# Fold amid block 8's products, an earlier load into its place, and four batches stored as whole rows

## Chip, cores and metric

One core of one Trainium2 chip runs the whole program. Time is device microseconds (us) of one execution; lower is better. The kernel before takes 438.74 us (median of three runs, 438.12 to 438.96).

## The reference

Three stages, all float32. x is 8 batches x 8 heads x 512 tokens x 64, state has 32 slots for each batch and head. Cut to what matters:

```python
# 1. attention both ways between tokens and state slots
a  = softmax(x @ state.T / 8);  xread = a @ state
a2 = softmax(state @ x.T / 8);  sread = a2 @ x
x  = concat([xread, sread], axis=2)          # 544 rows a batch, 4352 in all, 512 wide
# 2. dense layer
x = silu(x @ w_in) @ w_out                   # 512 -> 2048 -> 512
# 3. soft mixture: 8 experts x 4 slots
logits = x @ phi
d = softmax(logits, axis=0)                  # over all 4352 rows
slot_in = d.T @ x                            # 32 slots
slot_out[e] = relu(slot_in[e] @ w1[e]) @ w2[e]
out = softmax(logits, axis=1) @ slot_out     # 4352 x 512
```

The last softmax over rows and the slots need every row, so the experts run after the last block, and the result after the experts.

## The kernel before

**Blocks.** Blocks 0 to 7 are one batch's 512 tokens each; block 8 is the 256 state rows. For each block `hid` (or `hid8`, block 8) makes the hidden layer in pieces of 128 columns (tiles `h` in PSUM), ACT applies SiLU, `logits` or `logits8` multiplies with a folded matrix `w2p` (tile `lg`), and `s_rep`, `s_dTg` add the block's weighted hidden rows (`S`) into the sum `acc`, 128 x 4 x 512 in SBUF. In block 8 the weights come as high and low parts `wc`, made piece by piece by ACT, DVE and POOL from `win`, and the products are `h <- wc, rd`; `gt` are its transposes for `logits8`.

**The joint.** `join7` finds the minimum over rows after block 7 (tile `top`) and puts its factor into `r4e[:, 0]`. `sum7` scales the sum (tile `sum`). `fold` multiplies `acc` by `r4e` into 128 x 512 (four products, eight matmul records), and ACT copies it to `accX`. `rep8` does block 8's minimum (`lg8t`), exp (into `thb`) and transposes (`dT`). Then `slot_acc`, `slot_T` and `slot_mm` (tiles `siT`, `si`) make the slots' input from `accX` and block 8's `S`.

**Experts.** `f` are the products with w1 (two passes), `hT` their transposes, `so` the products with w2, once for each half of the 512 result columns. 32 tiles of 1 MB, 16 of w1 and 16 of w2, are loaded into places that earlier work leaves: `places` lists them (raw blocks, `win`, `g`, `acc`, `wb`, ...), `at_place` says which tile goes where, and `load_w(n)` issues the loads up to number n. `acc` is place 12. In `at_place` it holds tile 17, the second one of w2, and is loaded after `fold`.

**Result.** For each half of the columns `sor` is made from `so`, and `out_tiles` multiplies it with the softmax weights `cT` (tiles `o`, four for each batch), copies them to SBUF (DVE the even, ACT the odd), and `store` sends a batch out. `HALVES` are the batches whose first 256 columns are stored while the second half's `so` is still at work: all nine, so each batch leaves as two stores with rows of 1 KB (`outb[q, 0:512, cols]`).

**Order.** No engine runs in the order in which the code is written. `Recorder` records each instruction; `schedule` plays them through with planned durations and always takes the one of least priority number (place in the code plus `nc.shift` plus a number of the table `RANK`). SP issues all transfers in one queue, in that planned order, and at most eight are under way: an issue waits until the transfer eight before it has landed. In two stretches (`FILL`) the planner puts dummy products of `cst` into gaps of TensorE.

Of the kernel before, what the change touches and what calls it, by code (L numbers as in the profile page):

```python
# [15 lines left out]
NB = 8  # L16
# [30 lines left out]

LATE = {"in_w_out": 3.0, "wo_f32": 3.0, "in_xT_dr": 1.5, "in_xk_dr": 1.5}

LG8 = -450  # L50
FOLD = 0
# [18 lines left out]
HALVES = (0,1,2,3,4,5,6,7,NB)  # L70
# [44 lines left out]
    ("7", "ACT", "activation", "m", 0): 581,  # L115
    ("7", "ACT", "activation", "thb", 1): 1500,
    ("7", "ACT", "activation", "wo", 1): -857,
    ("7", "DVE", "transpose", "src", 0): 73,
    ("7", "DVE", "transpose", "src", 1): 200,
    ("7", "DVE", "transpose", "src", 3): 30,  # L120
    ("7", "DVE", "transpose", "src", 6): 1181,
    ("7", "PE", "matmul", "h", 8): 565,
    ("7", "PE", "matmul", "lg", 2): 1500,
    ("7", "PE", "matmul", "lg", 12): 1028,
    ("7", "PE", "matmul", "wbp", 0): 1474,
    ("7", "PE", "matmul", "wbp", 2): 615,
    ("8", "ACT", "copy", "wc", 5): -507,
    ("8", "DVE", "tensor_copy", "g", 0): -62,
    ("8", "DVE", "tensor_copy", "place", 0): -366,
    ("8", "DVE", "tensor_copy", "thb", 2): 991,  # L130
    ("8", "PE", "matmul", "S", 5): -333,
    ("8", "PE", "matmul", "dT", 0): 1251,
    ("8", "PE", "matmul", "f", 11): 823,
    ("8", "PE", "matmul", "f", 13): -209,
    ("8", "PE", "matmul", "h", 3): 119,
    ("8", "PE", "matmul", "h", 9): -974,
    ("8", "PE", "matmul", "h", 14): -745,
    ("8", "PE", "matmul", "lg", 4): 1500,
    ("8", "PE", "matmul", "o", 5): -14,
    ("8", "PE", "matmul", "o", 7): 948,  # L140
    ("8", "PE", "matmul", "si", 1): -1389,
    ("8", "PE", "matmul", "si", 2): -1381,
    ("8", "PE", "matmul", "si", 3): -562,
    ("8", "PE", "matmul", "so", 18): -193,
    ("8", "PE", "matmul", "so", 19): -442,
    ("8", "PE", "matmul", "so", 23): -570,
    ("8", "PE", "transpose", "dT", 0): 1161,
    ("8", "PE", "transpose", "gt", 9): 1042,
    ("8", "PE", "transpose", "gt", 10): 1014,
    ("8", "PE", "transpose", "hT", 0): 827,  # L150
# [69 lines left out]
class Recorder:  # L220
# [189 lines left out]
    def schedule(self):  # L410
# [44 lines left out]
        while n_left:  # L455
# [48 lines left out]
            if e == PE and any(lo <= busy[PE] < hi for lo, hi in FILL):  # L504
                at = max(busy[PE], self.filling[1])
                n = int((st - at - (0.2 if fills else 2.2)) / FILLER)
                room = []
                for tag in free:
                    if tag.split("_")[1] == "ps" and tag[0] != "h" and free[tag] and qpos[tag] < len(queue[tag]):
                        room.append((*min(free[tag]), tag))  # L510
                if n > 0 and room and min(room)[0] <= at:
                    _, old, tag = min(room)
                    order.append(self.filler(queue[tag][qpos[tag]], old, n, at))
                    fills += 1
                    mode, run = FULL, 0
# [8 lines left out]
            elif e == SP:  # L524
                op.start = st
                busy[SP] = st + op.cost
                t0 = max(st + op.cost + 0.9, dma_free)
                dma_free = t0 + op.bytes / DMA_RATE
                end = dma_free + 1.1
                landed.append(end)  # L530
                end += op.tail
            else:
                if e == ACT and op.mode is not None and table not in op.mode:
                    st += 1.3
                    table = op.mode[0]
                op.start = st
                busy[e] = st + op.cost
                end = st + op.cost + op.tail
                if e == DVE:
                    tailed = op  # L540
                    if op.port:
                        busy["port"] = end
                end += 0.04
# [66 lines left out]
def tile_state_attention_soft_moe(  # L610
# [557 lines left out]
    def rep8():  # L1168
# [5 lines left out]
        nc.after(fold_op[0], mm(p[:, 0:256], lhsT=r44, rhs=x, start=True, stop=True))  # L1174
# [110 lines left out]
    at_place = [0, 1, 2, 3, 4, 5, 6, 7, 8, 10, 9, 11, 13, 14, 15, 16, 17, 12, 18, 19, 20, 21, 22, 23] + [0, 1, 2, 3, 4, 5, 6, 8]  # L1285
# [41 lines left out]
    fold_op = []  # L1327

    def fold():

        p = bank("h", "fold")
        with nc.together():
            for q in range(4):
                op = mm(p[32 * q:32 * q + 32, :], lhsT=r4e[:, 0], rhs=acc[:, q], start=True, stop=True)
        fold_op[:] = [op]
        x = rot.tile([128, 512], F32, tag="wf", name="accX", bufs=1)
        nc.scalar.copy(out=x, in_=p)
        return x
# [178 lines left out]
    for fq in range(4):  # L1517
        hid8(fq)
        if fq == 0:
# [15 lines left out]
            s_dTg(NB - 1)  # L1535
            nc.shift = 0
# [4 lines left out]
        if fq == 1:  # L1541
# [6 lines left out]
            load_w(12)  # L1548
        if fq == 2:
            for n in range(12, 16):  # L1550
                split_w(n)
            load_w(13)
        if fq:
            logits8(fq - 1)
    load_w(16)
    logits8(3)
    load_w(17)
# [3 lines left out]

    nc.shift = FOLD
    accX = fold()
    load_w(18)
# [143 lines left out]
    todo = [*HALVES, *(q for q in range(NB + 1) if q not in HALVES)]  # L1708
# [56 lines left out]
```

## Time and profile before

| | us |
|---|---|
| median of three runs (lowest, highest) | 438.74 (438.12, 438.96) |
| the profiled execution, its time | 438.37 |
| its span, first to last instruction | 436.6 |
| TensorE busy (PE) | 414.4 (95%) |
| VectorE (DVE) | 291.9 (67%) |
| ScalarE (ACT) | 283.7 (65%) |
| GpSimd (POOL) | 119.2 (27%) |
| HBM read, written | 79.37 MB, 12.06 MB |

All numbers below come from this one execution. PE is the matmuls and PEld the loads of their weights. SPq is SyncE's queue of transfers, the time at which it issues one; "to landing" runs from there until the data is there. A matmul product in float32 shows as two records. The chain of waits follows the work that ended last back from the end; each piece is the time until the next piece takes over. PEclk is TensorE's granted clock as a share of 2.4 GHz. `L571` is the helper line that issues every instruction, so the tiles' names tell the instructions apart.

### The profile page before, as it was taken

What the parts mean: (1) busy time and instruction counts of PE and PEld (TensorE: products, weight loads), DVE (VectorE), ACT (ScalarE), POOL (GpSimd) and SP (SyncE); (2) the same over time, 40 slices, a digit from 0 to 9 for tenths busy, and PEclk for the clock granted to TensorE, in tenths of its full rate; (3) what the DMA queues carried; (4) which work ended last, traced back from release to release, by engine and by line L of the source; (5) the groups of instructions that cost most, each with busy time, mean ns of one, the idle gap of its engine ahead of it and who ended that gap; (6) DMA issues with size and microseconds to landing.
All of it is one profiled execution on the core that took longest, in us unless ns stands there. A gap on an engine that the chain in (4) does not pass through costs nothing.

```text
span 436.6 us, 10970 instructions
## 1 busy us (share of the span) xinstructions
PE 414.4 (95%) x4536; PEld 273.3 (63%) x4536; DVE 291.9 (67%) x548; ACT 283.7 (65%) x512; POOL 119.2 (27%) x71
## 2 busy tenths in 40 slices
PE   8889999999999999999999999999999999999980
PEld 5555657766856775785776677577677685435530
DVE  3989999883797598479659748943965544221460
ACT  4999997756688788679777657666876455011360
POOL 0024332044137135434714511441353130000000
PEclk9999999999999999999999999999999999999996
DMA  8999941238779998888896767465699988999998
GB/s 324 425 423 424 376 150 65 98 73 197 212 224 262 244 269 262 225 250 255 251 257 216 183 189 210 100 141 139 218 417 331 340 345 313 421 426 427 401 381 284
DMA packets 37890, 117.31 MB, mean 269 GB/s; under 512 B 3408, under 2 KB 12496, under 8 KB 29776
## 3 DMA queue, kind: packets, MB, share of 16 engines
q1 hardware_dynamic: 37840, 116.60, 79.3%
q8 instruction: 36, 0.59, 0.5%
q14 instruction: 14, 0.11, 0.1%
HBM read 79.37 MB, written 12.06 MB: 209 GB/s over the span
## 4 chain that ended last, share of the span: by engine, by line
PE 81%; DMA 8%; ACT 6%; DVE 2%; issue 0%; DVEq 0%; SPq 0%
PE h L571 44%; PE lg L571 7%; PE S L571 6%; PE wbp L571 6%; DMA raw<-in_w_in_dram 4%; PE so L571 3%; PE f L571 3%; DMA src<-in_w_out_dram 2%; PE o L571 2%; PE eT L571 1%; PE sc L571 1%; PE sr L571 1%; ACT L571 1%; DMA xT<-in_xT_dram 1%; PE si L571 1%; ACT g L571 1%
## 5 line engine op out<-in xcount | busy, mean ns | idle before, releaser
L571 PE MATMUL h<-ar,wb 128*128 128x512 f32 x768 | 189.6, 399 | 2.0 <-ACT g L571 2.0
L571 PEld LDWEIGHTS h<-ar,wb 128*128 128x128 f32 x768 | 140.2, 188 | 47.4 <-ACT g L571 6.4
L571 DVE STREAM_TRANSPOSE src<-g 128x512 f32<-128x512 f32 x112 | 78.0, 703 | 36.9 <-ACT g L571 31.9
L571 ACT ACTIVATE g<-h 128x512 f32<-128x512 f32 x100 | 58.9, 610 | 28.4 <-PE h L571 24.8
L571 POOL TENSOR_TENSOR wb<-wf,wb 128x512 fp32r<-128x512 f32 x26 | 33.8, 1299 | 111.4 <-ACT wb L571 89.7
L571 ACT CAST wb<-wbp 128x512 fp32r<-128x512 f32 x64 | 35.5, 594 | 10.4 <-PE wbp L571 9.6
L571 PEld LDWEIGHTS lg<-g,w2p 128*32 128x32 f32 x1072 | 28.1, 109 | 21.2 <-issue 16.8
L571 PE MATMUL lg<-g,w2p 128*32 128x128 f32 x1072 | 37.2, 275 | 0.2 <-DVE g L571 0.2
L571 POOL TENSOR_TENSOR s<-s,tm 128x1024 f32<-128x1024 f32 x12 | 23.3, 1941 | 43.0 <-DVE tm L571 35.9
L571 PE MATMUL wbp<-win,ss 64*32 64x512 f32 x512 | 33.3, 597 | 1.5 <-DVE win L571 1.1
L571 PE MATMUL S<-dst,dT 128*32 128x512 f32 (+1 forms) x328 | 28.4, 595 | 0.0
L571 ACT ACT_TABLE_LOAD x21 | 26.9, 1283 | 1.1 <-PEq L1755 0.7
L571 DVE TENSOR_TENSOR wb<-wbp,wb 128x512 fp32r<-128x512 f32 x38 | 24.9, 662 | 2.5 <-ACT wb L571 2.5
L571 ACT ACTIVATE thb<-h 128x512 f32<-128x512 f32 x30 | 17.9, 600 | 12.4 <-PE h L571 12.0
L571 DVE SCALAR_TENSOR_TENSOR g<-thb,h 128x512 f32<-128x512 f32 x28 | 18.9, 680 | 7.9 <-ACT thb L571 6.0
L571 PE MATMUL h<-wc,rd 128*128 128x512 f32 x96 | 24.0, 401 | 0.0
L571 DVE SCALAR_TENSOR_TENSOR acc<-acc,m,S 128x512 f32<-128x512 f32 x28 | 20.4, 736 | 4.3 <-PE S L571 3.8
L571 PE MATMUL lg<-thb 128*128 128x256 f32 x72 | 19.3, 415 | 1.2 <-DVE thb L571 1.2
L571 DVE TENSOR_REDUCE tm<-s 128x32 f32<-128x1024 f32 (+1 forms) x18 | 19.5, 1090 | 1.0 <-ACT s L571 0.8
L571 PEld LDWEIGHTS h<-wc,rd 128*128 128x128 f32 x96 | 17.5, 188 | 4.0 <-issue 0.2
L571 DVE TENSOR_REDUCE asm<-e 128x2 f32<-128x1024 f32 x8 | 9.6, 1203 | 15.3 <-ACT e L571 15.3
L571 PEld LDWEIGHTS lg<-thb 128*128 128x128 f32 x72 | 14.2, 205 | 5.7 <-issue 2.5
(190 smaller groups left out, 600.7 us busy)
## 6 DMA issues: line engine op xcount, KB each, us to landing
dst<-src SPq DMA_DIRECT2D x96, 256.0 KB, 4.8
place<-in_w_dram SPq DMA_DIRECT2D x12, 1024.0 KB, 9.6
xT<-in_xT_dram SPq DMA_DIRECT2D x8, 1024.0 KB, 8.6
raw<-in_w_in_dram SPq DMA_DIRECT2D x8, 1024.0 KB, 11.8
xk<-in_xk_dram SPq DMA_DIRECT2D x8, 1024.0 KB, 8.2
raw<-in_w_outT_dram SPq DMA_DIRECT2D x8, 1024.0 KB, 8.4
src<-in_w_out_dram SPq DMA_DIRECT2D x6, 1024.0 KB, 8.4
dst<-in_w_dram SPq DMA_DIRECT2D x6, 1024.0 KB, 12.3
```

Of the source, the lines that this page charges most:

```text
L571: made = [call(*args, **kwargs) for call, args, kwargs in op.calls]
```

## The change

`FOLD`, the shift that put `fold` after block 8, goes. `fold` is now recorded within `hid8`'s first round, after `s_dTg(NB - 1)`, and in the PSUM bank tag `w` instead of `h`. `at_place` exchanges two entries, so that `acc` holds tile 11 (of w1) and is loaded with the pieces of `win`; the tiles behind it move up by one place, and the numbers of `load_w` follow. `HALVES` becomes batches 0 to 3 and the state rows' part NB. In the planner a free stretch after 100 us is filled with dummies up to its end, and loads of over 0.9 MB after 250 us are planned to take 3 us longer. `RANK` has other numbers for blocks 7 and 8 (36 entries become 20).

```diff
+REST = 3.0
-FOLD = 0
-HALVES = (0,1,2,3,4,5,6,7,NB)
+HALVES = (0, 1, 2, 3, NB)
...
-    ("8", "PE", "transpose", "hT", 0): 827,
+    ("8", "PE", "matmul", "top", 0): 868,
...
-                n = int((st - at - (0.2 if fills else 2.2)) / FILLER)
+                n = int((st - at + 0.1) / 0.43) if st > 100 else int((st - at - (0.2 if fills else 2.2)) / FILLER)
...
-                t0 = max(st + op.cost + 0.9, dma_free)
+                t0 = max(st + op.cost + 0.9 + REST * (op.bytes > 9e5 and not op.tail and st > 250), dma_free)
...
-        nc.after(fold_op[0], mm(p[:, 0:256], lhsT=r44, rhs=x, start=True, stop=True))
+        mm(p[:, 0:256], lhsT=r44, rhs=x, start=True, stop=True)
...
-    at_place = [0, 1, 2, 3, 4, 5, 6, 7, 8, 10, 9, 11, 13, 14, 15, 16, 17, 12, 18, 19, 20, 21, 22, 23] + [0, 1, 2, 3, 4, 5, 6, 8]
+    at_place = [0, 1, 2, 3, 4, 5, 6, 7, 8, 10, 9, 12, 11, 13, 14, 15, 16, 17, 18, 19, 20, 21, 22, 23] + [0, 1, 2, 3, 4, 5, 6, 8]
...
     def fold():
-        p = bank("h", "fold")
+        p = bank("w", "fold")
...
             s_dTg(NB - 1)
+            nc.shift = -6 * FIRST
+            accX = fold()
             nc.shift = 0
...
-    nc.shift = FOLD
-    accX = fold()
-    load_w(18)
...
-    todo = [*HALVES, *(q for q in range(NB + 1) if q not in HALVES)]
+    todo = [*HALVES[:2], *(q for q in range(NB + 1) if q not in HALVES), *HALVES[2:]]
```

TensorE after block 7's part of S (not shown), in block 8, before; `h` are the hidden products, in threes:

```order
L571 MATMUL top_697<-fin,cst 128x4
L571 MATMUL h_1_1_707<-wc_677,rd 128x512 x3
L571 MATMUL h_1_1_707<-wc_686,rd 128x512 x6
L571 MATMUL gt_0_0_710<-cst,dst 128x128 x4
L571 MATMUL gt_0_1_711<-cst,dst 128x128 x4
L571 MATMUL h_2_0_714<-wc_677,rd 128x512 x3
L571 MATMUL h_2_1_715<-wc_677,rd 128x512 x3
L571 MATMUL gt_1_0_716<-cst,dst 128x128 x2
L571 MATMUL sum_708<-fin,cst 128x1
```

And in the same place now:

```order
L556 MATMUL h_1_1_709<-wc_686,rd 128x512 x3
L556 MATMUL h_1_0_708<-wc_686,rd 128x512 x3
L556 MATMUL h_1_1_709<-wc_686,rd 128x512 x3
L556 MATMUL top_697<-fin,cst 128x4
L556 MATMUL gt_0_0_712<-cst,dst 128x128 x4
L556 MATMUL gt_0_1_713<-cst,dst 128x128 x4
L556 MATMUL h_2_0_716<-wc_677,rd 128x512 x3
L556 MATMUL fold<-acc,r4e 32x512 x4
L556 MATMUL h_2_0_716<-wc_677,rd 128x512 x3
L556 MATMUL sum_710<-fin,cst 128x1
```

`fold` stands between products of `h_2_0`, and `top`, on which its factor rests, comes nine products later after S than before.

SP's queue at the end of the loads into `win`, before:

```order
L571 DMA win_80<-in_w_dram 128x512 x3
L571 DMA win_81<-in_w_dram 128x512 x4
L571 DMA place_724<-in_w_dram 128x2048
L571 DMA place_725<-in_w_dram 128x2048
L571 DMA place_726<-in_w_dram 128x2048
...
L571 DMA w2p<-in_w_dram 128x512
L571 DMA acc<-in_w_dram 128x2048
```

And now:

```order
L556 DMA win_80<-in_w_dram 128x512 x2
L556 DMA acc<-in_w_dram 128x2048
L556 DMA win_81<-in_w_dram 128x512 x4
L556 DMA place_726<-in_w_dram 128x2048
L556 DMA place_727<-in_w_dram 128x2048
L556 DMA place_728<-in_w_dram 128x2048
```

The load into `acc` moved ahead of eleven other loads.

TensorE from the second round of `so` to the first results of the last half, now (before, five pieces of `so_806` stood between 36 tiles `o` of the first half):

```order
L556 MATMUL o_0_3_789<-thb,win_79 64x256
L556 MATMUL so_790<-place_660,src 32x256 x8
L556 MATMUL so_790<-place_661,src 32x256 x8
L556 MATMUL so_790<-place_687,src 32x256 x8
L556 MATMUL so_790<-win_78,src 32x256 x8
L556 MATMUL so_790<-src 32x256 x16
L556 MATMUL sor_792<-sos_791,cst 128x256
L556 MATMUL o_256_0_793<-thb,win_79 128x256
```

The 20 tiles `o` of the first half all stand ahead of the last 48 products of `so`. After them come two half batches, then batches 4 to 7 as whole rows (`o` of 128x512, stores of `128x4x512`, 2 KB a row), then the other halves.

## Rows read from the trace of the kernel before

**Rows 1.** Page, part 2: mean busy share of the transfer engines in 40 slices

```profile
DMA  8999941238779998888896767465699988999998
```

**Rows 2.** Windows: length; PE, PEld, DVE, ACT, POOL busy; PEclk, transfer share, GB/s

```profile
357.00:366.00 9.00, 8.35 (x99) 6.71 (x98) 2.38 (x4) 3.64 (x6) 0.00 (x0) 1.00 0.70 239
360.00:361.00 1.00, 1.00 (x6) 0.77 (x6) 0.00 (x0) 0.15 (x1) 0.00 (x0) 1.00 0.01 4
361.00:362.00 1.00, 1.00 (x8) 0.86 (x7) 0.00 (x0) 0.34 (x1) 0.00 (x0) 1.00 0.88 197
378.00:408.00 30.00, 28.99 (x354) 12.60 (x350) 7.10 (x13) 5.25 (x12) 0.00 (x0) 1.00 1.01 425
410.00:411.00 1.00, 1.00 (x23) 0.64 (x24) 1.00 (x4) 0.69 (x3) 0.00 (x0) 1.00 0.98 366
411.00:432.00 21.00, 12.83 (x156) 5.65 (x144) 9.56 (x27) 8.85 (x27) 0.00 (x0) 0.92 1.09 382
```

**Rows 3.** Timeline of SP's queue: start us, us spent issuing, what

```profile
360.25 5.92 SPq L571 DMA_DIRECT2D place<-in_w_dram  x6
...
367.75 0.39 SPq L571 DMA_DIRECT2D acc<-in_w_dram  x1
...
404.64 0.40 SPq L571 DMA_DIRECT2D out_dram<-win  x1
...
419.67 0.42 SPq L571 DMA_DIRECT2D out_dram<-acc  x1
```

**Rows 4.** Transfers issued in 393 to 394 and 419 to 420: size, us to landing

```profile
src<-in_w_dram SPq DMA_DIRECT2D x1, 1024.0 KB, 19.4
...
out_dram<-acc SPq DMA_DIRECT2D x1, 512.0 KB, 5.7
```

**Rows 5.** Chain of waits after block 8's products: start us, us, what

```profile
361.62 1.53 PE gt L571 x14
...
365.89 0.70 PE lg8t L571 x2
366.59 1.00 PE fold L571 x8
367.58 0.80 PE dT L571 x6
```

**Rows 6.** Chain of waits from the last products to the results

```profile
395.14 6.22 PE so L571 x112
...
403.03 1.14 PE o L571 x14
...
406.03 1.07 PE o L571 x14
...
414.19 1.00 PE so L571 x16
```

**Rows 7.** Timeline of PE where block 7's logits stand

```profile
312.76 1.06 PE L571 MATMUL lg<-g,w2p 128*32 128x128 f32 x32
313.64 2.76 PE L571 MATMUL S<-dst,dT 128*32 128x512 f32 x24
...
329.42 2.06 PE L571 MATMUL lg<-g,w2p 128*32 128x128 f32 x64
331.40 6.57 PE L571 MATMUL h<-wc,rd 128*128 128x512 f32 x27
```

**Rows 8.** Timelines of DVE, ACT and PE around the joint

```profile
346.28 0.74 DVE L571 SCALAR_TENSOR_TENSOR acc<-acc,m,S 128x512 f32<-128x512 f32 x1
...
346.71 1.28 ACT L571 ACT_TABLE_LOAD   x1
...
367.09 0.47 ACT L571 ACTIVATE thb<-lg8t,m 128x256 f32<-128x256 f32 x1 [1.25 <-DVE m L571]
...
368.08 0.31 PE L571 MATMUL dT<-cst,thb 32*128 32x32 f32 x2
```

**Rows 9.** Transfers in 353 to 357.5: packets by size, rate

```profile
DMA packets 808, 1.78 MB, mean 395 GB/s; under 512 B 90, under 2 KB 90, under 8 KB 758
```

## Prediction before the run

> **What bounds the kernel now.** I read the transfer line of the page's 40 slices first [rows 1]: the queues are full from about slice 34 to the end, so the last 70 us are as much a question of bytes as of TensorE. The windows [rows 2] say it in numbers. From 378 to 408 the queue is full and moves 425 GB/s, all of it weights. It drops to 366 GB/s at 410, and from 411 to 432 it is full at 382 GB/s: those are the stores, whose packets are 1 KB. So weights end at about 410.2, and the whole result, 4352 x 512 x 4 bytes = 8.91 MB, follows without a hole: 8.91/0.382 = 23.3 us, to 433.5. The span ends 3.1 us later. Before that there is one hole: 357 to 366 moves only 239 GB/s, and 360 to 361 nearly nothing.
>
> Next I asked whether the stores wait for TensorE or for the queue. The first store of the second column half is issued at 419.67 [rows 3] and lands 5.7 us later, at 425.4 [rows 4]. The first half's stores (eight of 0.524 MB, and 0.262 MB for the last 256 rows) are 4.46 MB, 11.7 us, and keep the queue busy until 410.2 + 11.7 = 421.9. So the second half arrives about 2 us before it is needed, less about 1 us from issue to first byte. **The kernel ends on the queue, but TensorE stands only 1 us behind.** TensorE itself has no long gap on the way: its chain goes from gt to lg8t, fold and dT [rows 5] and, through so and o, to the second half [rows 6].
>
> **The change part by part.** The sum is made on the profiled execution, 438.37 us (span 436.6); the median of the three timed runs is 0.37 us above it, and I add differences to that median, 438.74.
>
> 1. *The load into acc.* It is issued at 367.75 [rows 3], after fold has read acc. In the new order it stands behind the win_80 pieces, so it comes into the hole of rows 2, which is worth 9 x (1 - 239/425) = 3.9 us. 1.05 MB at 425 GB/s is 2.5 us. The loads behind it wait for block 8's last products, which come later by what TensorE gains in work (point 2), about 1.2 us. Weights then end at 410.2 - 2.5 + 1.2 = 408.9. The last src load now lands 19.4 us after its issue at about 393 [rows 4], and so1 needs it only at about 412, so TensorE isn't held by it. This part alone brings the queue's end forward by 1.3 us.
>
> 2. *fold amid block 8.* Its eight matmuls take 1.00 us [rows 5]. Between lg8t and dT part of that lay under the wait for DVE's minimum and ACT's exp; amid h products nothing waits, so it is all added: +1.0 (0.9 to 1.1). A gain is excluded, since the eight matmuls are the same. In the old place, dT on thb stands behind it and starts at 368.08, though the exp that makes thb is done at 367.09 + 0.47 = 367.56 [rows 8]: at best 0.52 us comes back. But two dummy products S<-cst now stand there, of the shape of lg8t, which takes 0.70 us with its latency [rows 5]; two can fill all that fold leaves free. I take -0.2, bounds 0 and -0.52.
>
> 3. *Another excursion of lg.* The block-7 logits now interrupt the products twice instead of once. In a run of the same tile shape 32 lg matmuls take 313.64 - 312.76 = 0.88 us; 64 between products take 331.40 - 329.42 = 1.98 [rows 7]. So one excursion costs 1.98 - 1.76 = 0.22: +0.2 (0 to 0.3).
>
> 4. *The new wait of fold.* It needs r4e, so the joining minimum top. In before, DVE reduces top between the first and second addition into acc; now all four additions (0.74 each) stand ahead, and on ACT two casts stand ahead of the exp. Behind that exp a table load of 1.28 us [rows 8] stands ahead of the copy of fold's result, and sum, on TensorE three products later, needs the bank that this copy frees. Queued behind a waiting fold are the h products, and so everything. No row shows this wait: bounds 0 (the work ahead covers it) and 0.8 (one addition too many). I take +0.2, near the lower end: between S and fold TensorE has twelve h matmuls of 6.57/27 = 0.24 [rows 7] and eight gt of 1.53/14 = 0.11 [rows 5], 3.8 us, against four additions and some small steps, about 4.
>
> The other dummies (one before lg8t, one more before si) lie in gaps of about 0.4 us that are there now: 0, at most +0.2. The granted clock is 1.00, the level of 2.4 GHz, in every window up to 411 [rows 2], so there is none to win back. TensorE's shift is 1.0 - 0.2 + 0.2 + 0.2 = **+1.2 us**, bounds +0.4 and +2.2.
>
> 5. *Fewer results in the first half.* Between the halves' products stand now 20 o tiles, not 36. Put together from rows 6: 403.03 + seven o 1.14 + so 1.00 + seven o 1.07 + so 1.00 + six o 0.92 + 96 so at 6.22/112 each, 5.33 = 413.5, against 415.2 (the last so starts at 414.19 and takes 1.00). From so's end to the first store was 3.27 us in the first half (401.37 to 404.64, rows 3 and 6); so the last half's first store is issued at 416.8 + 1.2 = 418.0. From issue to first byte on an empty queue: a load issued at 360.25 [rows 3] moves 4 GB/s until 361 and 197 in the next microsecond [rows 2], so 0.9 to 1.4; I take 1.1. First byte: **419.1**.
>
> 6. *What the queue has until then.* Only four half batches and the small rows: 2.36 MB, 6.2 us, to 408.9 + 6.2 = 415.1. **So the queue runs dry for about 4 us**, which it doesn't do now, and the end no longer depends on the acc load at all. After 419.1 it has 6.55 MB to move: 2.36 MB in 1 KB rows (6.2 us) and 4.19 MB in 2 KB rows.
>
> 7. *Whole rows.* The nearest rows are the 256 KB pieces of win, nearly all packets between 1 and 8 KB in 353 to 357.5: 395 GB/s [rows 9]. That lies between 382 for 1 KB and 425 for 8 KB, and I take it: 4.19/0.395 = 10.6 us, 0.4 less than at 382 (bounds 0 and 1.1). The Trainium skill, page "DMA: Bandwidth & Descriptors", section "Specifications", puts the smallest transfer for line rate at 512 B, so 1 KB and 2 KB would do equally well. By that rule the 0.4 is not there and the time is 0.4 us longer; rows 2 and 9 speak against it, since the rate rises from 382 over 395 to 425. TensorE and the copies aren't the bound there: a whole batch is two copies of 128x512 on each of DVE and ACT, about 1.4 us, against 2.6 us on the queue.
>
> Sum: data ends at 419.1 + 6.2 + 10.6 = 435.9 against 433.5: **+2.4 us, 441.1**. With the low ends (shift 0.4, first byte after 0.9, 425 GB/s) it is +0.7, 439.4; with the high ends (2.2, 1.4, 382) +4.1, 442.8.
>
> **Rivals.** *The queue stays the bound (faster).* If the last half's stores are there before the queue is dry, the end is 410.2 - 2.5 + 6.2 + 6.2 + 10.6 = 430.7, -2.8 us, 435.9. It decides from a first byte at 415.8 on, 3.4 us earlier than I have it: then the gain is over 0.9 us. For it speaks that the queue is full now and has 1 us in hand; against it, that so1 can't end before 413.5 without any shift. The Trainium skill, page "DMA: Bandwidth & Descriptors", section "Rules for kernel authors", advises to issue a DMA early and wait for it late, which would promise this; the hole in rows 2 agrees that early issue has room, but not that the end follows.
>
> *TensorE hides the fold (no change).* If fold, the extra excursion and the wait cost nothing on balance, and whole rows reach the rate of loads: 416.8 + 0.9 + 6.2 + 9.9 = 433.8, +0.3, 439.0. For it: small gaps on TensorE may not show in modelled ends. Against: the chain of rows 5 has none before the end of h.
>
> *The early load comes late (slower still).* If acc isn't free in the hole, src lands at 412.3 + 1.2 and so1 waits about 1.5 us for it: 442.6.
>
> **How the numbers follow.** The forecast has 0.66, the faster rival 0.14, no change 0.14, the late load 0.06. About 0.2% (0.9 us) is what a measurement of this kernel can tell from no change. Slower: 0.66 + 0.06 and a quarter of the no-change case, 0.75; same 0.11; faster 0.14. The range leaves out the faster rival below 438.0 and what lies over 442.6, which needs all the high ends at once or the late load.
>
> **What would show it.** Right: the acc load issued before 358 and no hole of rows 2's size; so ending at 414 to 415.5; a hole of 3 to 5 us in the queue between 414 and 420; then 6.5 MB at 380 to 400 GB/s to about 436. Wrong: no hole there, the first whole-row store issued before 416, TensorE's h products ending at 361.6 as now, or whole rows at over 425 GB/s.

## The result and the profile after

The changed kernel takes 440.40 us (median of five runs, 440.24 to 440.71); the kernel before, beside it, 438.67. The ratio of the times, after over before, is **1.0051, 95% interval 1.0037 to 1.0066**: slower by 2.2 us (1.6 to 2.9). The profiled execution took 440.24 us, its span is 438.5. The forecast was 441.1 and +2.4.

The page of after, part 2 (DMA is the busy share of the transfer engines in tenths, over 40 slices of the span), answers to [rows 1]:

```profile
DMA  8999941238778998897895867564898989999988
GB/s 316 423 428 420 363 158 70 97 75 195 212 224 261 251 287 235 241 275 235 244 269 183 189 189 197 126 156 106 301 411 319 349 346 338 386 419 425 364 303 312
```

Before, slices 35 to 39 moved 421, 426, 427, 401 and 381 GB/s. Now they move 386, 419, 425, 364 and 303: a hole has opened close to the end. The windows (length; PE, PEld, DVE, ACT, POOL busy; PEclk, transfer share, GB/s) answer to [rows 2]:

```profile
357.00:366.00 9.00, 8.84 (x96) 7.30 (x98) 3.62 (x6) 3.37 (x6) 0.00 (x0) 1.00 0.82 275
361.00:362.00 1.00, 1.00 (x6) 0.81 (x5) 0.00 (x0) 0.00 (x0) 0.00 (x0) 1.00 0.07 27
...
415.00:420.00 5.00, 3.50 (x38) 1.83 (x34) 2.31 (x6) 2.00 (x6) 0.00 (x0) 1.00 0.47 164
420.00:435.00 15.00, 4.72 (x44) 1.59 (x40) 6.58 (x14) 5.58 (x14) 0.00 (x0) 0.77 1.05 387
```

The hole at 360 is smaller (275 GB/s over 357 to 366 where it was 239) and a new one stands at 415 to 420. At 382 GB/s, the rate of the stores before, it is worth 5 x (1 - 164/382) = 2.9 us. The queue does not stop at once: in the four microseconds from 415 it moves 260, 163, 83 and 37 GB/s. SP's queue (start us, us spent issuing, what) says why, and answers to [rows 3]:

```profile
350.64 0.33 SPq L556 DMA_DIRECT2D acc<-in_w_dram  x1
...
409.68 3.96 SPq L556 DMA_DIRECT2D out_dram<-place  x3
418.32 0.39 SPq L556 DMA_DIRECT2D out_dram<-win  x1
```

The load into `acc` is issued 17 us earlier than before. The first half's stores are all issued by 413.6, the next one, the first store of the last half, only at 418.32, when `sor` and the first copies of the last half are there. TensorE's chain of waits (start us, us, what), which answers to [rows 5] and [rows 6]:

```profile
362.44 1.75 PE gt L556 x16
...
366.44 0.63 PE dT L556 x2
367.07 0.56 PE lg8t L556 x2
...
367.99 0.94 PE S L556 x4
...
373.04 1.06 PE f L556 x4
374.10 3.64 PE si L556 x64
...
404.32 1.14 PE o L556 x14
...
408.53 1.22 PE o L556 x12
409.75 5.36 PE so L556 x96
415.11 0.02 issue
```

`dT L556 x2` at 366.44, `S L556 x4` and `f L556 x4` are dummies (two records for each product); one of the two `f` stood in before too. The last `so` ends at 415.11. The chain behind it goes straight to the first copies and the store of 418.32: TensorE now sets the end, through an idle queue.

**One common point for all traces.** When block 6's `S` starts differs from execution to execution: in the fourteen traces it lies between 310.84 and 312.32 us, in no order by kernel. The three e_joint kernels below, in which TensorE does the same work in the same order until after 365 us, start it at 310.84, 311.32 and 312.32. It was 311.88 in the profiled execution of before and 311.46 in that of after, so after had a head start of 0.42 us there. From that point on TensorE's times agree between traces within 0.05 us wherever the programs are the same and the clock stays up. So I read TensorE's shift from there. The timelines of PE (start us, us, what), of before and then of after:

```profile
311.88 1.06 PE L571 MATMUL S<-dst,dT 128*32 128x512 f32 x8
...
361.46 1.69 PE L571 MATMUL gt<-cst,src 128*128 128x128 f32 x14
...
368.74 1.07 PE L571 MATMUL S<-dst,dT 128*32 128x512 f32 x8
```

```profile
311.46 3.64 PE L556 MATMUL S<-dst,dT 128*32 128x512 f32 x32
...
362.28 1.91 PE L556 MATMUL gt<-cst,src 128*128 128x128 f32 x16
...
369.58 1.07 PE L556 MATMUL S<-dst,dT 128*32 128x512 f32 x8
```

`gt` after block 8's products starts 49.58 us after block 6's `S` in before and 50.82 in after, block 8's `S` 56.86 and 58.12. (In after and the kernels made from it two of the `gt`, 0.22 us, stand in this last group and not earlier, x16 against x14, so their column `gt` shows 0.2 less than TensorE has lost; block 8's `S` comes behind the same work in all.) The same reading of every trace stands in this table (us after the start of block 6's `S`; `sor` is the product that ends the first half):

| trace | gt | S of block 8 | sor | ratio to before, 95% |
|---|---|---|---|---|
| before | 49.58 | 56.86 | 89.93 | 1 |
| after | 50.82 | 58.12 | 91.64 | 1.0051 (1.0037 to 1.0066) |
| e_only_five | 49.59 | 56.87 | 89.96 | 1.0030 (1.0018 to 1.0041) |
| e_nine | 50.85 | 58.16 | 91.67 | 1.0031 (1.0020 to 1.0042) |
| e_seven | 50.84 | 58.14 | 91.66 | 1.0041 (1.0028 to 1.0054) |
| e_two_stores | 50.84 | 58.15 | 91.66 | 1.0073 (1.0060 to 1.0087) |
| e_acc_late | 50.85 | 58.16 | 91.67 | 1.0064 (1.0045 to 1.0083) |
| e_no_fill | 50.85 | 58.16 | 92.52 | 1.0061 (1.0041 to 1.0082) |
| e_nine_no_fill | 50.85 | 58.24 | 92.79 | 1.0048 (1.0032 to 1.0063) |
| e_no_f_fill | 50.87 | 58.18 | 91.43 | 1.0046 (1.0029 to 1.0062) |
| e_old_fill | 50.87 | 58.18 | 91.43 | 1.0045 (1.0029 to 1.0060) |
| e_joint | 50.77 | 57.87 | 92.42 | 1.0015 (1.0001 to 1.0029) |
| e_joint_no_fill | 50.79 | 57.88 | 90.86 | 1.0027 (1.0011 to 1.0042) |
| e_joint_s_fill | 50.79 | 57.88 | 90.86 | 1.0013 (0.9998 to 1.0027) |

The experiments were timed in three groups, each beside the kernel before: e_only_five, e_nine, e_seven and e_two_stores (before 438.11 us), e_acc_late and the three without any late dummy (438.05), the other four (438.27). Since before's median moves from group to group, kernels of different groups are compared by the ratio; 0.1% is 0.44 us.

### The profile page after: what moved, and what is told of

Read it like the earlier page. It is cut to its first block, busy times and chain, and to the rows that moved or that the text cites. A ratio compares the mean times of both kernels' runs of the same rounds, so it can differ in the third digit from the quotient of the medians.

```text
span 438.5 us, 10890 instructions
## 1 busy us (share of the span) xinstructions
PE 414.2 (94%) x4512; PEld 273.6 (62%) x4512; DVE 292.4 (67%) x540; ACT 282.7 (64%) x504; POOL 119.1 (27%) x71
## 4 chain that ended last, share of the span: by engine, by line
PE 85%; DMA 5%; ACT 5%; DVE 1%; issue 0%; SPq 0%; DVEq 0%
PE h L556 45%; PE S L556 7%; PE lg L556 7%; PE wbp L556 6%; DMA raw<-in_w_in_dram 4%; PE f L556 3%; PE so L556 3%; PE o L556 2%; PE eT L556 1%; PE sr L556 1%; PE sc L556 1%; DMA ss<-in_stT_dram 1%; ACT L556 1%; PE si L556 1%; ACT win L556 1%; PE gt L556 1%
## 5 line engine op out<-in xcount | busy, mean ns | idle before, releaser
L556 PE MATMUL h<-ar,wb 128*128 128x512 f32 x768 | 189.9, 399 | 2.0 <-ACT g L556 2.0
L556 PEld LDWEIGHTS h<-ar,wb 128*128 128x128 f32 x768 | 140.1, 188 | 47.6 <-ACT g L556 7.3
L556 DVE STREAM_TRANSPOSE src<-g 128x512 f32<-128x512 f32 x112 | 78.1, 704 | 38.1 <-ACT g L556 31.5
L556 ACT ACTIVATE g<-h 128x512 f32<-128x512 f32 x100 | 59.0, 610 | 28.5 <-PE h L556 26.8
L556 POOL TENSOR_TENSOR wb<-wf,wb 128x512 fp32r<-128x512 f32 x26 | 33.7, 1297 | 109.3 <-ACT wb L556 88.6
L556 ACT CAST wb<-wbp 128x512 fp32r<-128x512 f32 x64 | 35.4, 593 | 9.4 <-PE wbp L556 8.6
L556 PEld LDWEIGHTS lg<-g,w2p 128*32 128x32 f32 x1072 | 28.1, 109 | 20.8 <-issue 16.6
L556 PE MATMUL lg<-g,w2p 128*32 128x128 f32 x1072 | 37.1, 275 | 0.2 <-DVE g L556 0.2
L556 POOL TENSOR_TENSOR s<-s,tm 128x1024 f32<-128x1024 f32 x12 | 23.3, 1939 | 42.2 <-DVE tm L556 37.6
L556 PE MATMUL wbp<-win,ss 64*32 64x512 f32 x512 | 32.9, 596 | 1.1 <-DVE win L556 1.1
L556 PE MATMUL S<-dst,dT 128*32 128x512 f32 (+1 forms) x328 | 28.2, 595 | 0.0
L556 DVE TENSOR_TENSOR wb<-wbp,wb 128x512 fp32r<-128x512 f32 x38 | 25.0, 665 | 2.6 <-ACT wb L556 2.5
L556 ACT ACTIVATE thb<-h 128x512 f32<-128x512 f32 x30 | 17.9, 600 | 11.6 <-PE h L556 11.1
L556 PE MATMUL h<-wc,rd 128*128 128x512 f32 x96 | 24.3, 401 | 0.0
L556 DVE SCALAR_TENSOR_TENSOR g<-thb,h 128x512 f32<-128x512 f32 x28 | 18.9, 682 | 7.9 <-ACT thb L556 6.0
L556 DVE SCALAR_TENSOR_TENSOR acc<-acc,m,S 128x512 f32<-128x512 f32 x28 | 20.3, 738 | 3.8 <-PE S L556 3.3
L556 PEld LDWEIGHTS h<-wc,rd 128*128 128x128 f32 x96 | 17.5, 188 | 5.6 <-issue 1.0
L556 PE MATMUL lg<-thb 128*128 128x256 f32 x72 | 19.3, 415 | 1.2 <-DVE thb L556 1.2
L556 DVE TENSOR_REDUCE tm<-s 128x32 f32<-128x1024 f32 (+1 forms) x18 | 19.5, 1091 | 1.0 <-ACT s L556 0.8
L556 DVE TENSOR_REDUCE asm<-e 128x2 f32<-128x1024 f32 x8 | 9.6, 1203 | 14.2 <-ACT e L556 14.2
L556 PEld LDWEIGHTS lg<-thb 128*128 128x128 f32 x72 | 14.2, 205 | 5.7 <-issue 2.5
```

Source lines behind the costliest of these rows:

```text
L556: made = [call(*args, **kwargs) for call, args, kwargs in op.calls]
```

## The experiments

### The output alone, and the rest of the change without it

**e_only_five** is the kernel before with only the new list of batches:

```diff
-HALVES = (0,1,2,3,4,5,6,7,NB)
+HALVES = (0, 1, 2, 3, NB)
-    todo = [*HALVES, *(q for q in range(NB + 1) if q not in HALVES)]
+    todo = [*HALVES[:2], *(q for q in range(NB + 1) if q not in HALVES), *HALVES[2:]]
```

> The kernel before with one edit: only batches 0 to 3 and the state rows' part are stored in the first half, batches 4 to 7 as whole rows in the last. fold and the load into acc stay where they were. Theory (the queue runs dry): no shift of TensorE, so ends at about 413.5, the last half's first store is issued at 416.8, the queue is dry from about 416.4 to 417.9, and 6.55 MB after it take 16.8 us: data end 434.7, +1.2 us, 439.8. Rival (what costs is fold and the other work of TensorE amid block 8): no change, 438.7. Third (whole rows are a gain of their own): 438.2.

Measured 439.55 us, ratio 1.0030: +1.3 us. TensorE is not shifted at all (the table). Its windows, and its first store of the last half:

```profile
415.00:420.00 5.00, 3.65 (x34) 1.63 (x33) 3.06 (x8) 2.37 (x7) 0.00 (x0) 1.00 0.62 216
420.00:435.00 15.00, 4.32 (x40) 1.59 (x40) 5.83 (x13) 4.83 (x12) 0.00 (x0) 0.79 1.05 386
```

```profile
417.57 0.39 SPq L571 DMA_DIRECT2D out_dram<-win  x1
```

The store comes 2.1 us earlier than the 419.67 of [rows 3], because 16 fewer `o` tiles stand ahead of it. But four half batches, 2.1 MB, are missing from the queue in the meantime, and it runs dry: 216 GB/s for 5 us, worth 2.2 us, part of which the whole rows give back (e_two_stores, below). A shorter path to the last half's first store made the kernel slower.

In after that store stands 418.32 - 311.46 = 106.86 us behind block 6's `S`, in e_only_five 417.57 - 311.83 = 105.74. The output is the same in both; the rest of the change makes the store 1.1 us later, and the ratio rises by 0.0021, 0.9 us: with the queue dry, the end goes with TensorE.

**e_nine** and **e_seven** are the changed kernel with more first halves: all nine, and batches 0 to 5 with the state rows.

```diff
-HALVES = (0, 1, 2, 3, NB)
+HALVES = (0, 1, 2, 3, 4, 5, 6, 7, NB)
...
```

```diff
-HALVES = (0, 1, 2, 3, NB)
+HALVES = (0, 1, 2, 3, 4, 5, NB)
```

> The changed kernel with the output put back: all nine first halves are stored while the second half's so is at work, no whole rows. fold, the load into acc and the dummies stay as changed. Theory: TensorE stays 1.3 us behind, but the queue has 4.46 MB to store until then and is dry for 1 us at most; the last half's first byte comes at about 421 to 422 and 4.46 MB take 11.7 us: data end 433 to 433.8, total 438.6 (437.9 to 439.2). Rival (TensorE's added work is the whole cost): 440.4 or later, since TensorE ends later with more tiles between.

> The changed kernel with batches 4 and 5 stored in halves too, so batches 0 to 5 and the state rows in the first half and only 6 and 7 as whole rows. Theory: each batch moved ends so 0.65 us later and takes 1.3 us of bytes from what is left after it, as long as the queue is dry: 1.3 us less for two, 439.1, and a hole of about 2.7 instead of 4 us. Rival (TensorE's work is the cost): 440.4. If the hole is no cause, later so makes it slower: 441.7.

Measured 439.65 (1.0031) and 439.85 (1.0041), by the ratio +1.4 and +1.8 us. Expected were 438.6 and 439.1, which against 438.67 is -0.1 and +0.4: both are 1.4 us slower than expected. The order is the expected one, but the two intervals overlap. e_nine lies outside its range (439.2 is a ratio of 1.0012), and its rival, 440.4 or a ratio of 1.0039, lies inside its interval. So the old output takes about 0.9 us (0.0020) off the cost of the change, and 1.4 remain without any whole rows. The windows of e_nine, its first store of the last half, and the rate behind it, of e_nine and then of before:

```profile
411.00:420.00 9.00, 7.99 (x112) 3.65 (x109) 2.92 (x8) 2.89 (x9) 0.00 (x0) 1.00 1.08 380
420.00:423.00 3.00, 2.32 (x32) 1.21 (x29) 2.28 (x7) 2.00 (x7) 0.00 (x0) 1.00 0.82 266
```

```profile
421.35 0.39 SPq L556 DMA_DIRECT2D out_dram<-win  x1
```

```profile
423.00:432.00 9.00, 3.41 (x40) 1.60 (x40) 4.14 (x12) 3.71 (x12) 0.00 (x0) 0.92 1.07 369
```

```profile
423.00:432.00 9.00, 1.65 (x24) 0.58 (x16) 2.52 (x8) 2.22 (x8) 0.00 (x0) 0.82 1.09 382
```

With the old output a hole is left (266 GB/s for 3 us, worth 0.9 us). TensorE's shift at `sor` is not the 1.3 us by which the two profiled executions differ there but 1.7, since the head start hides 0.4; and the first store of the last half is 2.2 us late (421.35 - 311.33 = 110.02 against 419.67 - 311.88 = 107.79; where the last 0.5 of it arises was not traced). The expectation had counted 1.3 us. With the about 1 us that the queue had in hand by the prediction, 1.2 us of the 2.2 are left, near the 1.4 measured. The stores behind the hole move 369 GB/s over 423 to 432 where before moves 382, another 0.3 us; why is not settled. In e_seven the hole is smaller than in after, as expected: 356, 221, 69 and 335 GB/s in the four microseconds from 417, worth 1.4 us.

**e_two_stores** is the changed kernel in which each whole batch leaves as two stores of half the size with rows of 1 KB; nothing else moves.

```diff
-            nc.sync.dma_start(
-                out=outb[q, 0:512, cols].rearrange("(t p) f -> p t f", p=128), in_=obuf[q][:, :, cols]
-            )
+            for c in range(cols.start, cols.stop, 256):
+                at = slice(c, c + 256)
+                nc.sync.dma_start(
+                    out=outb[q, 0:512, at].rearrange("(t p) f -> p t f", p=128), in_=obuf[q][:, :, at]
+                )
```

> The changed kernel with each of the four whole batches sent as two stores of 256 columns, 1 KB a row, one behind the other; nothing else differs. If the rate goes with the row's size (382 GB/s for 1 KB, some 395 to 400 for 2 KB), 4.19 MB take 0.4 to 0.5 us more: 440.8. If rows of 1 KB and 2 KB move equally well: 440.4. The time to first byte and the hole stay the same in both.

Measured 441.40, ratio 1.0073. The same windows as above, of this kernel:

```profile
415.00:420.00 5.00, 3.50 (x38) 1.82 (x34) 2.34 (x6) 2.03 (x6) 0.00 (x0) 1.00 0.41 143
420.00:435.00 15.00, 4.69 (x44) 1.59 (x40) 6.54 (x14) 5.55 (x14) 0.00 (x0) 0.79 1.07 371
```

The hole is nearly the same (143 against 164 GB/s, 0.3 us of bytes, which are missing before the first whole batch leaves). Behind it 371 instead of 387 GB/s move. Both figures hold stores of half batches too; from 426 to 430 whole batches alone are on the way, in after and then in e_two_stores:

```profile
426.00:430.00 4.00, 0.06 (x4) 0.00 (x0) 0.84 (x3) 0.73 (x3) 0.00 (x0) 0.78 1.05 409
```

```profile
426.00:430.00 4.00, 0.02 (x3) 0.00 (x0) 0.81 (x3) 0.69 (x3) 0.00 (x0) 0.84 1.09 385
```

By the ratios (0.0022 x 438) whole batches with rows of 2 KB are worth 1.0 us here, though the two intervals overlap a little; by the rates from 420 on it is 0.6 us. The edit halves the rows and doubles the number of stores at once, so which of the two slows the queue is not shown. The Trainium skill, page "DMA: Bandwidth & Descriptors", section "Specifications", puts the smallest transfer for line rate at 512 B; this pair of kernels speaks against that, as far as it is the rows: 385 GB/s with 1 KB, 409 with 2 KB.

### The load into acc

**e_acc_late** is the changed kernel with the fold where it is, but the load back near its old place in the queue, behind the pieces of `win` (issued at 365.11; in before at 367.75, behind two more loads into `place` and `w2p`):

```diff
-    at_place = [0, 1, 2, 3, 4, 5, 6, 7, 8, 10, 9, 12, 11, 13, 14, 15, 16, 17, 18, 19, 20, 21, 22, 23] + [0, 1, 2, 3, 4, 5, 6, 8]
+    at_place = [0, 1, 2, 3, 4, 5, 6, 7, 8, 10, 9, 11, 13, 14, 15, 16, 17, 12, 18, 19, 20, 21, 22, 23] + [0, 1, 2, 3, 4, 5, 6, 8]
...
-                    nc.sync.dma_start(out=t, in_=src)
+                    op = nc.sync.dma_start(out=t, in_=src)
+                    if places[at_p] == "acc":
+                        nc.after(op, *exps[NB + 2])
...
```

> The changed kernel with the fold where the change puts it, but the load into acc in its old place in the queue (places exchanged back; issued behind the loads into win and place). Theory (the queue is dry before the last half in any case, so its being 1.3 us ahead is worth nothing): weights end about 411 instead of 408.7, the hole before the last half shrinks by as much, and the end stays: 440.4, ratio 1.0051 (1.0045 to 1.0060). Rival one (so waits for the last weights): so1 ends up to 0.8 us later, ratio up to 1.007. Rival two (the early load itself disturbs other traffic and delays TensorE): ratio under 1.004.

Measured 440.79, ratio 1.0064; that is just above the expected range, and the interval holds the changed kernel's 1.0051. The windows at the end of the weights, of this kernel and then of after:

```profile
408.00:411.00 3.00, 3.00 (x49) 1.41 (x44) 1.61 (x5) 1.45 (x5) 0.00 (x0) 1.00 1.00 421
415.00:420.00 5.00, 3.50 (x38) 1.82 (x34) 2.18 (x6) 1.87 (x6) 0.00 (x0) 1.00 0.73 255
```

```profile
408.00:411.00 3.00, 3.00 (x49) 1.36 (x45) 1.47 (x4) 1.32 (x5) 0.00 (x0) 1.00 0.99 359
```

With the late load the weights' rate of 421 GB/s lasts until 411, in after it is over by 409. What the early load gains, the hole takes: 255 GB/s with the late load, 164 with the early one. The first store of the last half stands 106.90 us behind block 6's `S` against 106.86, so `so` doesn't wait for the late load (rival one), and the spans differ by 0.2 us. The early load, for which the fold was moved, is worth at most what this comparison can't resolve: the ratio's interval reaches from 1.0045 to 1.0083.

### Fold and dummies

**e_no_fill** and **e_nine_no_fill** are the changed kernel, with five and with nine first halves, without the dummies in the late stretch.

```diff
-FILL = ((0.0, 60.0), (355.0, 383.0))
+FILL = ((0.0, 60.0),)
```

> The changed kernel without the dummy products of cst in the late stretch (one dT, two S, two f); all else stays. Theory (the dummies ahead of si stand in the path, since si starts 1.44 us later than before while S of block 8 starts only 0.84 later): si starts 0.4 to 0.6 us earlier against the start of block 8's S, everything up to the first store of the last half comes earlier by as much, and since the queue is dry there the end follows: about 439.9, ratio to before 1.0037 (1.0030 to 1.0045). Rival one (they only fill a wait for slotT, as the prediction had it): si starts as now, ratio 1.0051. Rival two (they keep the clock up): TensorE's granted clock falls below 1.00 between 366 and 380 and the time rises, ratio 1.006 or more.

> The changed kernel with all nine first halves stored early (as before) and without the late dummies. Theory (with nine halves the queue is barely dry, and the end follows TensorE's shift): the run with nine halves and dummies gave 1.0031, this one 0.4 to 0.6 us less, 1.0020 (1.0013 to 1.0027). Rival (with nine halves the end hangs on the queue's rate, not on TensorE): 1.0031 as with the dummies.

Measured 440.93 (1.0061) and 440.15 (1.0048). Both ratios lie above those with dummies (1.0051 and 1.0031), though the intervals overlap; both theories, a gain of 0.4 to 0.6 us, missed. The second rival of the first expectation holds in the trace: the clock fell. PE's timeline of e_no_fill (in brackets the idle time before, and who ended it), and its window:

```profile
366.84 0.70 PE L556 MATMUL lg8t<-lg8s,cst 128*128 128x256 f32 x2 [0.49 <-ACT lg8s L556]
...
368.66 0.30 PE L556 MATMUL dT<-cst,thb 32*128 32x32 f32 x2 [0.75 <-ACT thb L556]
369.12 0.45 PE L556 MATMUL siT<-accX,r4e 32*32 32x128 f32 x16 [0.15 <-DVE r4e L556]
369.50 1.61 PE L556 MATMUL S<-dst,dT 128*32 128x512 f32 x8
370.87 1.95 PE L556 MATMUL S<-src,dT 128*32 128x512 f32 x8
```

```profile
370.00:374.00 4.00, 4.00 (x64) 1.10 (x56) 2.52 (x10) 1.25 (x3) 0.00 (x0) 0.59 1.02 375
```

In after the same window, 370 to 374, has a granted clock of 1.00, and the two groups of `S` take 1.07 and 1.04 us. Here, behind waits of 0.49, 0.75 and 0.15 us, the clock is 0.59 on average, so for most of the window at the lower level of 1.2 GHz, and `S` takes 1.61 and 1.95. The trace of e_nine_no_fill shows the same (0.60). `sor` comes 0.88 us later than in after. Not every execution is hit: of e_no_fill's six runs three have a granted clock of 0.983 or 0.984 over the span and take 441.00 to 441.23 us, the traced one among them, and three have 0.989 and take 440.23 to 440.87.

**e_no_f_fill** leaves out only the two dummies `f<-cst` ahead of `si`; **e_old_fill** takes the rule of before (which gives one `S` and one `f` here).

```diff
-FILL = ((0.0, 60.0), (355.0, 383.0))
+FILL = ((0.0, 60.0), (355.0, 368.0))
```

```diff
-                n = int((st - at + 0.1) / 0.43) if st > 100 else int((st - at - (0.2 if fills else 2.2)) / FILLER)
+                n = int((st - at - (0.2 if fills else 2.2)) / FILLER)
```

> The changed kernel without the two dummy products f<-cst ahead of si alone; the dummies dT and S stay. The run without any late dummy had si at its old place and S of block 8 twice as long at a granted clock of 0.67. Theory (the dummies ahead of lg8t and dT keep the clock up, those ahead of si only stand in the way): granted clock 1.00 from 365 to 380, si starts 0.3 to 0.45 us earlier than with them, ratio 1.0042 (1.0035 to 1.0050). Rival (the clock needs those two as well): clock falls below 1.00 between 370 and 380, ratio 1.0055 or more.

> The changed kernel with the rule for dummies of before: one S and one f, not one dT, two S, two f. Theory: one S dummy of 0.5 us in the wait of 1.3 us for thb holds the clock as it does in the kernel before; si starts 0.2 us earlier than in the changed kernel; ratio 1.0047 (1.0038 to 1.0055). Rival (one is too few): clock below 1.00 in part of 366 to 375 in some runs, wide spread, ratio 1.0055 or more.

Measured 440.18 (1.0046) and 440.08 (1.0045). Both keep the clock at 1.00 in the profiled run, and `sor` comes 0.21 us earlier than in after in both. So the `dT`, the second `S` and one `f` cost nothing that shows; the second `f` ahead of `si` costs 0.2 us. The difference of the ratios (0.0005) lies inside the intervals, so the time alone doesn't show it; the table does.

**e_joint_no_fill**, **e_joint** and **e_joint_s_fill** are the kernel before with the fold and the load moved, its own table of order numbers and all nine first halves. They differ in the late dummies alone: none, the rule of before (one `S`, one `f`), and one `dT` and two `S` with none ahead of `si`.

```diff
+            nc.shift = -6 * FIRST
+            accX = fold()
             nc.shift = 0
...
-    nc.shift = FOLD
-    accX = fold()
...
-FILL = ((0.0, 60.0), (355.0, 383.0))
+FILL = ((0.0, 60.0),)
```

The last two lines are those of e_joint_no_fill; e_joint is without them, and e_joint_s_fill has (355.0, 368.0) there and the change's rule for the number of dummies.

> The kernel before with the fold and the load into acc moved as in the change, but with the table of order numbers of before, all nine first halves, and no late dummies: no second excursion of block 7's logits. Theory (the shift of TensorE is the fold 1.0, its wait 0.2, the excursion 0.26, the dummies 0.5, the joint -0.16): left are fold, wait and joint, about +0.7 to +1.0 us at the start of si against before, less the dummies that before has itself (about 0.2): the last half starts +0.5 to +0.8 late, ratio 1.0015 (1.0005 to 1.0022). Rival (what counts is the earlier load: the queue is 1.3 us ahead and the end follows it): 437.4, ratio 0.997.

> The kernel before with the fold and the load into acc moved as in the change, its own table of order numbers, nine first halves, and its own rule for dummies (one S, one f). Without dummies this kernel spread from 437.65 to 440.4, with granted clocks from 0.992 to 0.985 over the span. Theory (the spread is the clock falling in the wait for thb, in some runs): with the dummies the clock stays, the runs lie within 1 us, at 438.0, ratio 1.0000 (0.9985 to 1.0010). Rival (the fold's shift of TensorE costs 1 us here too): ratio 1.002 to 1.003.

> The same kernel as the one with its own dummies, but with the dummies of the change ahead of lg8t and dT (one dT, two S) and none ahead of si. Theory: the clock stays as with one S and one f, and si starts about 0.1 to 0.2 us earlier: ratio 0.9995 (0.998 to 1.0010), the fastest of the four. Rival (the queue sets the end, and weights end only as early as the last slice of products lets them): the same as with its own dummies.

Measured 439.37, 438.79 and 438.88 us; ratios 1.0027, 1.0015 and 1.0013. Expected were 1.0015, 1.0000 and 0.9995: all three lie above their ranges (up to 1.0022, 1.0010 and 1.0010), with intervals that reach into them. For e_joint_s_fill the rival holds, since it is no faster than e_joint. That the spread of the runs is the clock can be part of it at most: they lie between 437.65 and 440.40 without dummies, 438.16 and 439.78 in e_joint, and 438.09 and 440.76 in e_joint_s_fill, whose trace kept the clock. The granted clock in the window 370 to 374, of e_joint_no_fill, then of e_joint:

```profile
370.00:374.00 4.00, 3.82 (x85) 1.95 (x81) 2.52 (x7) 0.98 (x2) 0.00 (x0) 1.00 1.00 378
```

```profile
370.00:374.00 4.00, 4.00 (x65) 1.11 (x58) 2.29 (x9) 1.16 (x2) 0.00 (x0) 0.65 1.04 374
```

The kernel without dummies kept its clock in this execution and the one with two dummies lost it. So with these waits the clock can fall; whether it does differs from one execution to the next. With one `dT` and two `S` it fell in none of seven traces, with fewer or none in three of five; with so few traces chance isn't excluded.

Even the mildest form of the move is not a gain. In e_joint_s_fill, clock 1.00, `sor` is 0.93 us later than in before, and the first store of the last half comes at 420.92 - 312.32 = 108.60 us after block 6's `S` instead of 107.79. Its interval reaches down to 0.9998, so a cost isn't certain; a gain of the move is seen in none of the variants.

## Why the prediction was right, step by step

**The sum.** +2.4 us forecast, +2.2 (1.6 to 2.9) by the ratio. The predicted 441.1 lies 0.7 above the measured 440.40; the base gives 0.1 of that (438.74 forecast from, 438.67 beside this run). The mechanism held, but part of the hit is luck. At an equal start the first store of the last half is issued at 418.32 + 0.42 = 418.74, 0.7 later than the 418.0 of point 5. From there to the end of the span it takes 438.5 - 418.32 = 20.2 us, where the prediction had put together 1.1 + 6.2 + 10.6 + 3.1 = 21.0. The two misses cancel. The first is taken apart below; the second isn't traced to one term.

**Point 1, the load.** Right: issued at 350.64, and the end doesn't depend on it (e_acc_late). The hole at 360 was filled only partly, 275 GB/s instead of 239: the next loads into `place` are issued at 361.07 where it was 360.25, and 361 to 362 moves 27 GB/s.

**Points 2 to 4, TensorE until block 8's S.** Forecast +1.2; measured 58.12 - 56.86 = +1.26. The parts come apart by the table. e_joint_no_fill has the fold without the second excursion: +1.21 at `gt` (forecast 1.0 for the fold and 0.2 for its wait). It loses only 1.02 by block 8's `S`, so 0.19 comes back in the joint (forecast 0.2). The second excursion of `lg` is 58.16 - 57.88 = 0.28 (forecast 0.2).

The **cause** of one term was wrong. Point 4 booked 0.2 us for a wait of the fold. There is none, as the chain of after shows around it, with DVE's row for its factor:

```profile
347.95 0.93 PE gt L556 x8
348.88 0.70 PE h L556 x3
349.58 0.99 PE fold L556 x8
350.58 0.90 PE h L556 x3
```

```profile
348.69 0.24 DVE L556 TENSOR_SCALAR r4e<-cst,fin 128x32 f32<-128x32 f32 x1
```

`r4e` is done at 348.93, the fold starts at 349.58 behind products that never stop. The 0.2 us lie behind it: three `h` take 0.90 us after the fold and 0.70 before it. The difference is the overlap: in PE's timeline three `h` run about 0.95 us both times, but start 0.25 us before the last `gt` ends and only 0.07 before the fold does. The fold uses tiles of 128 x 32 of the array, `h` and `gt` 128 x 128, as in the excursions of `lg` [rows 7], which cost as much. That the change of tile is the reason is argued from this; no run changes the tile alone. The Trainium skill, page "TensorEngine Tiling (Array Packing)", section "Key Properties", says that a change of tiling mode drains TensorE. These rows agree, with 0.2 to 0.3 us for going there and back.

**The mis-sized term: the way from block 8's S to si.** I had put the dummies there at 0 (at most +0.2) and nothing else. Measured, `sor` is 91.64 - 89.93 = +1.71 late, 0.45 more than at `S`. The pieces, by the way from `S` to `sor` in the table, are the second dummy `f`, 0.27 (33.52 us in after, 33.25 in e_no_f_fill and also in e_old_fill, which has one `f`), and the table of order numbers, 0.27 (32.98 in e_joint_s_fill, which has before's table and no `f`); before itself takes 33.07. DVE's timelines of after and of e_joint_s_fill show the second:

```profile
370.74 0.69 DVE L556 COPY thb<-S 64x512 f32<-64x512 f32 x1
371.47 0.17 DVE L556 TENSOR_SCALAR cm<-cm 128x2 f32<-128x2 f32 x1
371.55 0.16 DVE L556 RECIPROCAL fin<-fin 128x1 f32<-128x1 f32 x1
371.68 0.17 DVE L556 RECIPROCAL cm<-cm 128x2 f32<-128x2 f32 x1
371.87 0.69 DVE L556 COPY thb<-S 64x512 f32<-64x512 f32 x1
```

```profile
371.61 1.30 DVE L571 COPY thb<-S 64x512 f32<-64x512 f32 x2
```

The new entry `("8", "DVE", "tensor_copy", "thb", 3): 180` stands for the second of two copies that `siT` waits for, and three small steps now run between them. No run changes this entry alone. The second copy ends 2.98 us after the start of block 8's `S` there and 2.71 in e_joint_s_fill. The bounds of the forecast, +0.4 and +2.2, held the 1.71. Between the two profiled executions only 1.71 - 0.42 = 1.29 is visible, which looks like the forecast of 1.2 by luck.

**Point 5, the first store.** Forecast 418.0, measured 418.32 with the head start, 418.74 without. Of the 0.7, 0.5 is TensorE's shift (1.71, not 1.2). The rest is the stretch from `so` to `so` with 20 tiles `o`: 415.11 - 402.65 = 12.46 us where I had put together 12.1, since the last six `o` took 1.22 us and not 0.92. From there to the store it was 3.2, as forecast.

**Point 6, the dry queue.** Right, and the core of the forecast: about 4 us were forecast, the hole is worth 2.9. No store is issued between 413.6 and 418.32, but those under way run out slowly (164 GB/s on average, not 0). e_only_five shows that the output part alone opens it. It is not the whole cause. By the forecast's reading the queue of before has 1 us in hand against a shift of 1.2, so the fold's part alone would cost next to nothing with the old output; e_nine shows a first store of the last half that is 2.2 us late, and 1.4 us of cost.

**Point 7, whole rows.** Forecast 395 GB/s [rows 9] and 0.4 us; measured 409 where the queue is full of them (426 to 430), 387 over the whole stretch, and 1.0 us against two stores with 1 KB rows. The direction held; the reason, the length of the rows, is not separated from the number of stores. The rate with 1 KB rows over the whole stretch was 371, below the 382 of before, which I had compared with.

**The rivals.** "The queue stays the bound" needed a first byte at 415.8; the store was issued at 418.32. "TensorE hides the fold" is refuted by the table, 1.0 us at block 8's `S` in the mildest form. "The early load comes late" is refuted by the chain: `so` has no wait before 415.11.

How the parts add: the output alone +1.3 (e_only_five), the rest with the old output +1.4 (e_nine), the whole change +2.2. They share the same hole, and each interval is about 0.5 us wide on either side, so the 0.5 us between sum and whole is not resolved. So the output is about half of the cost, and the fold with its dummies and its order about the other half.

## What to carry to other kernels

When a queue and an engine finish close together, ask of a change not only what it makes earlier, but how much work is left for the queue until the next piece is ready: here sending less early, in better rows, cost more than the rows gave. Moving work out of a wait into a full stretch cost all of its length here (1.2 us, of which 0.2 came back in the wait), and a load that it frees is worth nothing if the end doesn't hang on loads. Compare traces from a common point shortly before the changed place, or the variation of the executions passes for the effect.

## What the runs showed of the hardware that I had not expected

- Waits of 0.49, 0.75 and 0.15 us, in a kernel whose TensorE is else full, went with a granted clock of 0.59 instead of 1.00 (mean of 370 to 374), and block 8's `S` took 3.3 us instead of 1.9 from its start to its end. It happened in three of five traces without the full set of dummies and in none of seven with it, so a dummy in a wait can be worth more than its own time, and one execution does not tell.
- The same 4.2 MB as eight stores with rows of 1 KB or as four with rows of 2 KB differ by 1.0 us (385 and 409 GB/s where the queue holds nothing else).
- The time at which one point of the same program is reached, after 311 us of work, varies by 1.5 us between executions (310.84 to 312.32 in the three e_joint kernels). The effect that was studied is 2.2 us.
